# Sparse attention into a Swish feed-forward: batch 0 in two halves of queries, tiled scores and AV in every batch, block-mean rows copied by VectorE

## The chip, the cores and the metric

The program runs on one core of one Trainium2 chip. The metric is device time in microseconds (us) of one execution. Five instruction streams run side by side and meet through semaphores: TensorE (PE; its weight loads are shown apart as PEld), VectorE (DVE), ScalarE (ACT), GpSimd (POOL) and SyncE (SP). In this kernel POOL issues the loads from HBM, SP issues the copies inside SBUF, the transposes by DMA and the stores of the output; all of them share 16 DMA engines.

## The reference

Four batches, 8 heads, 768 positions, head dimension 64. Each query sees the keys nearer than 16 positions to it and, besides, 24 summary keys (the maximum over each block of 32 keys) whose values are the means over the blocks. The result goes through a feed-forward layer of 512 -> 2048 -> 512 with `h * sigmoid(beta * h)` between.

```
k_sum = k.reshape(B, H, nb, block, D).max(axis=3)        # block 32, nb 24
v_sum = v.reshape(B, H, nb, block, D).mean(axis=3)
scores_l = scale * q @ k.T                               # kept where |i - j| < 16
scores_s = scale * q @ k_sum.T + log(block)
a = softmax(concat([where(mask_l, scores_l, -1e9), scores_s]))
x = a @ concat([v, v_sum])                               # heads side by side: (3072, 512)
h = x @ w_in                                             # (3072, 2048)
out = (h / (1 + exp(-beta * h))) @ w_out                 # (3072, 512)
```

## The kernel before

**Tiling.** Two heads make a pair `g` (four pairs a batch). 64 queries and the 96 keys around them are one piece; a piece has 128 rows: 96 keys and, in 32 rows that the band leaves free, the 24 summary keys. Even and odd pieces (`par` 0 and 1) have their own images of K (`kw[:, 0]` and `kw[:, 1]`) and of V (`ve` and `vo`), shifted by 64 rows against each other. `vo` is a copy of `ve`, made by two DMAs of the SP queue (`copy_v`). The block means come from seven matmuls on `ve` (`prep_v`), are rounded into `vm`, and four DMAs a pair spread them into the free rows of `vo` and `ve` (L326). The two into `ve` have to wait until `copy_v` has read `ve`.

**Batch 0** runs before the feed-forward: for each pair its K and Q are transposed on TensorE (`prep_k`, `prep_q`), the block maxima are taken on VectorE (`rows_k`), then come the scores (L341 puts -30000 outside the band by a matmul with the identity, L345 adds q.k, two heads in the two 64-row halves of the array), the exponential on ScalarE, one pair later AV (L375, the odd pieces in the upper 64 columns of the array) and its normalisation (`norm0`), and two pairs later the transposition into `xT`. **Batches 1 to 3** do the same as side work of the batch before. There the two heads of a piece are kept apart by zeros in `q2`, so that a score piece is one matmul of 128x128 (L353), and AV is one of 128x130 (L380), half of whose output is not used; VectorE multiplies by the band (`mask`) and picks the valid halves in two instructions (L396). Batch 1 comes through TensorE transposes, batches 2 and 3 through DMA transposes (`cross`, and `rows_q` which spreads them into `q2`).

**Feed-forward.** Of each batch, 16 row tiles of the up projection (`h_tile`, eight matmuls of 384 columns each and one Silu), then six output tiles of the down projection in four parts of four matmuls (`o_part`). The weights are loaded once by POOL after the inputs of batch 0; `w_out` is scaled by 1/beta in 16 VectorE instructions (L225).

**What sets the order.** The program is written out by hand. Each engine executes in the order in which the instructions are emitted. The loop at the end keeps a list `main` (the feed-forward of batch b) and a list `side` of (position, function) with the attention of batch b+1; the side work is emitted before the entry of `main` whose number its position has reached. An engine whose next instruction waits lets nothing pass.

Of the kernel before, what the change touches and what calls it, by code (L numbers as in the profile page):

```python
# [12 lines left out]
def kernel(  # L13
# [10 lines left out]
    nc = tc.nc  # L24
# [54 lines left out]
    q2_bufs = [const.tile([P, nch, 2, 2, QT], bf16, name=f"q2{i}") for i in range(NKW)]  # L79
    qt_bufs = [const.tile([P, S], bf16, name=f"qt{i}") for i in range(2)]  # L80
# [39 lines left out]
    for g in range(2):  # L120
        load_hold("k", g, nc.sync)
        load_hold("q", g, nc.scalar)
# [6 lines left out]
    near = const.tile([P, 3, QT], bf16, name="near")  # L129
    nneg = const.tile([P, 3, QT], bf16, name="nneg")  # L130
    summ = const.tile([P, 1], f32, name="summ")
    band = const.tile([P, 2, nch, 2, QT], bf16, name="band")
    negband = const.tile([P, 2, nch, QT], bf16, name="negband")
# [18 lines left out]
    def clear_q(i):  # L152
        zero(q2_bufs[i][0:D, :, :, 1, :])
        zero(q2_bufs[i][D:P, :, :, 0, :])

# [6 lines left out]
    nc.vector.memset(A_col, 1.0 / block)  # L162
    make_identity(nc, identity)
    zero(A_avg)
    clear_v(0)
    select(A_col, -W, [[P, NC], [-block, nb]], 1)
    select(A_col, block - 1 + W, [[-P, NC], [block, nb]], -1)
    select(near, -1, [[0, 3], [-1, QT]], 1)
    select(near, 2 * W - 1, [[0, 3], [1, QT]], -1)
    select(near[:, 1], -W, [[0, QT]], 1)  # L170
    select(near[:, 2], D + W - 1, [[0, QT]], -1)
# [3 lines left out]
    load_v(0, 0)  # L175
    load_run("k", 0, 2)
    load_v(0, 1)
    load_run("q", 0, 2)
    load_v(0, 2)
    load_run("k", 0, 3)  # L180
    load_v(0, 3)
    load_run("q", 0, 3)

    nc.vector.tensor_copy(out=identity32[:], in_=identity[:])
    for t in vm_bufs:
        nc.vector.memset(t[:, :, D:VW], 1.0)
    clear_k(0)
    cast_hold("k", 0, nc.vector.tensor_copy)
    cast_hold("q", 0, nc.scalar.copy)
    clear_k(1)  # L190
    for s in SUM:
        nc.vector.tensor_copy(out=A_avg[:, :, s:s + nb], in_=A_col[:])
    nc.vector.tensor_scalar(out=near[:], in0=near[:], scalar1=summ[:, 0:1], scalar2=None, op0=ALU.max)
    nc.vector.tensor_scalar(out=bias[:, 0:1], in0=summ[:], scalar1=log_block, scalar2=None, op0=ALU.mult)
    nc.vector.tensor_scalar(out=nneg, in0=near, scalar1=1.0, scalar2=-NEG, op0=ALU.subtract, op1=ALU.mult)
    for lo, hi in ((0, D), (D, 0)):
        nc.vector.tensor_copy(out=bias[lo:lo + D, 1:2], in_=bias[hi:hi + D, 0:1])

    def spread(dst, src, bc):


        nc.vector.tensor_copy(out=dst[:, 0, 1:nch], in_=bc(src[:, 0], nch - 1))
        nc.vector.tensor_copy(out=dst[:, 0, 0:1], in_=bc(src[:, 1], 1))
        for lo, hi in ((0, D), (D, 0)):
            nc.vector.tensor_copy(out=dst[lo:lo + D, 1, 0:nch - 1], in_=bc(src[hi:hi + D, 0], nch - 1))
            nc.vector.tensor_copy(out=dst[lo:lo + D, 1, nch - 1:nch], in_=bc(src[hi:hi + D, 2], 1))

    spread(negband, nneg, lambda a, n: a[:, None, :].to_broadcast([a.shape[0], n, QT]))
# [12 lines left out]
    def make_band():  # L221
        spread(band, near, lambda a, n: a[:, None, None, :].to_broadcast([a.shape[0], n, 2, QT]))
# [46 lines left out]
    def prep_q(b, g, tag="t"):  # L269
        p = turn("q", b, g, tag)  # L270
        if b == 0:
            t = qt_bufs[g % 2]
            qt[(b, g)] = t
            nc.scalar.copy(out=t.rearrange("p (t j) -> p t j", j=J), in_=p.rearrange("p j t -> p t j"))
            return
        pv = p.rearrange("p j (m t) -> p m t j", t=QT // J)
        q2 = q2_bufs[(b * npair + g) % NKW].rearrange("p m r h (t j) -> p (m r) h t j", j=J)
        for h, copy in ((0, nc.scalar.copy), (1, nc.vector.tensor_copy)):
            copy(out=q2[h * D:(h + 1) * D, :, h], in_=pv[h * D:(h + 1) * D])  # L279

    def cross(b, g):
# [4 lines left out]
        qt[(b, g)] = qk_pool.tile([P, nch, P], bf16, name="q_tr", tag="q_tr")  # L286
        nc.sync.dma_start_transpose(out=qt[(b, g)][:], in_=qn.rearrange("p c h d -> p (c h d)"))

    def rows_k(b, g):
        kw = kw_of(b, g)  # L290
        cv = nc.vector.tensor_copy
        cv(out=kw[:, 1, 0:nch, 64:P], in_=kw[:, 0, 0:nch, 64:P])  # L292
        cv(out=kw[:, 1, 0:nch, 0:32], in_=kw[:, 0, 1:NC, 0:32])
        flat = kw[:, 0].rearrange("p c f -> p (c f)")[:, W:W + S].rearrange("p (n f) -> p n f", f=block)
        half = at_pool.tile([P, nb, block // 2], bf16, name="half", tag="half", bufs=2)
        nc.vector.tensor_max(out=half[:], in0=flat[:, :, 0:block // 2], in1=flat[:, :, block // 2:block])
        km = at_pool.tile([P, nb], bf16, name="km", tag="km")
# [160 lines left out]
    for i in range(2, NKW):  # L458
        clear_k(i)
# [122 lines left out]
```

## Time and profile before

| | us |
|---|---|
| median of 3 runs (lowest to highest) | 261.42 (260.54 to 261.93) |
| the profiled execution, its own time | 259.94 |
| its span in the trace | 258.1 |
| PE busy | 222.5 (86%) |
| ACT busy | 120.1 (47%) |
| DVE busy | 114.6 (44%) |
| POOL busy | 64.2 (25%) |

The span is the time from the first to the last instruction of the trace; the execution's own time has 1.84 us more around it. Busy time is the union of an engine's instructions. The page cuts the span into 40 slices of 6.45 us and gives a digit for each. The chain of waits follows the work that ended last backwards from instruction to releaser. It gives 68% to PE, 16% to DMA and 10% to DVE. By line it names the two projections (L427 30%, L442 27%), the spreading of the block means into `ve` (8%), AV of batches 1 to 3 (3%) and the copies of `ve` into `vo` (3%).

### The profile page before, as it was taken

How to read it: one execution, taken by the hardware profiler on the slowest of the kernel's cores; microseconds unless marked ns; L12 is line 12 of the kernel's file. 1: busy time of each engine (PE TensorE's matmuls, PEld its weight loads, DVE VectorE, ACT ScalarE, POOL GpSimd, SP SyncE). 2: the span in 40 equal slices, each digit the busy share in tenths (PEclk: the TensorE clock that was granted, in tenths of full speed). 3: DMA queues.
4: the chain of work that ended last, by engine and by line, in shares of the span. 5: the costliest groups of instructions: out<-in, count | busy, mean ns of one | idle time of the engine just before them, and what ended most of it. 6: DMA issues, size and time to landing. Idle time of an engine off the chain costs nothing.

```text
span 258.1 us, 4624 instructions
## 1 busy us (share of the span) xinstructions
PE 222.5 (86%) x1809; PEld 131.9 (51%) x1809; DVE 114.6 (44%) x324; ACT 120.1 (47%) x140; POOL 64.2 (25%) x90
## 2 busy tenths in 40 slices
PE   0495764289999889899996999999999999999994
PEld 0353543256566545456662665566655545664441
DVE  3932532068174887704335876062378720001221
ACT  2554404036788424146666433566675418662000
POOL 8962121740198620006638000000000000000000
PEclk9999955589999999999999999999999999999999
DMA  6999999999099957139999942565434441000122
GB/s 190 185 181 200 192 204 196 177 178 50 0 105 143 179 65 112 55 95 147 151 157 166 151 122 74 142 138 97 83 52 118 96 118 43 0 0 10 74 81 81
DMA packets 95669, 29.73 MB, mean 115 GB/s; under 512 B 83856, under 2 KB 91808, under 8 KB 95648
## 3 DMA queue, kind: packets, MB, share of 16 engines
q0 software_dynamic: 56768, 12.85, 59.9%
q1 hardware_dynamic: 38464, 15.81, 29.6%
q10 hardware_dynamic: 416, 0.79, 1.1%
q8 instruction: 14, 0.23, 0.4%
q14 instruction: 7, 0.06, 0.1%
HBM read 27.27 MB, written 6.29 MB: 130 GB/s over the span
## 4 chain that ended last, share of the span: by engine, by line
PE 68%; DMA 16%; DVE 10%; ACT 2%; issue 1%; SPq 1%; DVEq 0%; ACTq 0%
PE h_ps L427 30%; PE o_ps L442 27%; DMA ve<-vm 8%; PE av_ps L380 3%; DMA vo<-ve 3%; PE s_ps L353 2%; DMA kw<-k_nat 2%; DMA hold_k<-in_k_dram 2%; DVE x_nat L396 2%; DMA vo<-vm 2%; PE vm_ps L319 2%; PE av_ps L375 1%; DVE q L279 1%; DVE km L298 1%; PE px L411 1%
## 5 line engine op out<-in xcount | busy, mean ns | idle before, releaser
L442 PE MATMUL o_ps<-w_out_sb,h_sb 128*128 128x512 bf16 x384 | 89.3, 379 | 0.1
L427 PE MATMUL h_ps<-xT,w_in_sb 128*128 128x384 bf16 x512 | 86.8, 328 | 0.6 <-DVE xT L412 0.6
L431 ACT ACTIVATE h_sb<-h_ps,beta_sb 128x768 bf16<-128x768 f32 x64 | 57.1, 900 | 38.6 <-PE h_ps L427 38.5
L427 PEld LDWEIGHTS <-w_in_sb 128*128 128x128 bf16 x512 | 49.6, 98 | 33.3 <-issue 1.6
L442 PEld LDWEIGHTS <-h_sb 128*128 128x128 bf16 x384 | 35.9, 98 | 36.8 <-issue 0.3
L354 ACT ACTIVATE attn<-s_ps,bias 128x768 bf16<-128x768 f32 x24 | 21.4, 900 | 19.2 <-PE s_ps L353 16.2
L396 DVE TENSOR_TENSOR x_nat<-av_ps,r 64x384 bf16<-64x384 f32 x48 | 26.6, 555 | 1.2
L446 ACT COPY o_sb<-o_ps 128x512 f32<-128x512 f32 x18 | 10.5, 585 | 30.6 <-PE o_ps L442 25.6
L98 POOL DMA_DIRECT2D k_nat<-in_k_dram x16 | 13.4, 844 | 42.0 <-DMA kw<-k_nat 27.1
L446 DVE COPY o_sb<-o_ps 128x512 f32<-128x512 f32 x6 | 4.2, 692 | 41.8 <-issue 28.1
L292 DVE COPY kw<-kw 128x384 bf16<-128x384 bf16 x16 | 5.0, 313 | 36.3 <-DMA kw<-k_nat 33.4
L105 POOL DMA_DIRECT2D ve<-in_v_dram x16 | 17.0, 1060 | 5.8 <-DVE x_nat L387 2.7
L375 PE MATMUL av_ps<-ve,attn 128*64 128x65 bf16 x48 | 4.0, 240 | 12.4 <-DMA ve<-vm 12.4
L359 DVE TENSOR_TENSOR attn<-attn,band 128x768 bf16<-128x768 bf16 x24 | 13.3, 556 | 1.8 <-ACT attn L354 1.2
L380 PEld LDWEIGHTS <-attn 128*128 128x128 bf16 x144 | 10.1, 97 | 7.6 <-DVE attn L359 2.8
L98 POOL DMA_DIRECT2D q_nat<-in_q_dram x16 | 13.2, 837 | 2.9 <-DMA q_tr<-q_nat 2.6
L353 PE MATMUL s_ps<-q,kw 128*128 128x128 bf16 x144 | 11.9, 219 | 1.2 <-DVE x_nat L396 1.2
L261 PE MATMUL pk<-identity,k_run 96*64 96x96 bf16 x128 | 5.5, 244 | 8.4 <-DVE k_run L116 6.7
L375 PEld LDWEIGHTS <-attn 128*64 128x64 bf16 x96 | 5.3, 154 | 13.3 <-issue 12.3
L319 PE MATMUL vm_ps<-ve,A_avg 128*128 128x128 bf16 x112 | 10.4, 241 | 1.7 <-DMA ve<-in_v_dram 1.7
L267 ACT COPY kw<-pk 128x768 bf16<-128x768 bf16 x8 | 6.4, 796 | 11.0 <-PE pk L261 9.7
L347 ACT ACTIVATE attn<-s_ps,bias 128x768 bf16<-128x768 f32 x8 | 7.1, 899 | 8.9 <-PE s_ps L345 8.9
(76 smaller groups left out, 180.8 us busy)
## 6 DMA issues: line engine op xcount, KB each, us to landing
out_dram<-o_sb SPq DMA_DIRECT2D x24, 256.0 KB, 2.3
ve<-in_v_dram POOLq DMA_DIRECT2D x12, 192.0 KB, 7.0
w_in_sb<-in_moe_w_in_dram POOLq DMA_DIRECT2D x4, 512.0 KB, 14.8
w_out_sb<-in_moe_w_out_dram POOLq DMA_DIRECT2D x4, 512.0 KB, 22.3
vo<-ve SPq DMA_DIRECT2D x16, 97.5 KB, 5.4
k_nat<-in_k_dram POOLq DMA_DIRECT2D x16, 96.0 KB, 5.6
q_nat<-in_q_dram POOLq DMA_DIRECT2D x16, 96.0 KB, 5.6
k_run<-in_k_dram POOLq DMA_DIRECT2D x6, 192.0 KB, 8.5
```

The source lines that it names most:

```text
L98: nc.gpsimd.dma_start(out=t[:, :, h], in_=(k_row if nm == "k" else q_row)[b, g, :, h])
L105: nc.gpsimd.dma_start(out=ve_bufs[b % 2][:, lo:hi, 0:D], in_=src)
L319: nc.tensor.matmul(vm_ps[:], A_avg[:, c, :], ve[:, lo:lo + nch + 1:nch, 0:D], start=(c == 0), stop=(c == NC - 1))
L353: nc.tensor.matmul(sv[:, m // HM, m % HM], kw[:, m, :], q2[:, m, par], start=True, stop=True)
L354: nc.scalar.activation(out=a.rearrange("p (k j) h f -> p k (j h f)", k=2), in_=big[:, :, 0:w], func=ACTF.Exp, bias=bias[:, par:par + 1], s ...
L359: nc.vector.tensor_mul(out=a, in0=a, in1=band[:, par])
L380: nc.tensor.matmul(ov[:, m // HM, m % HM], a[:, m], vt[:, m:m + nch + 1:nch], start=True, stop=True)
L396: nc.vector.tensor_mul(out=x[par * QT:(par + 1) * QT, :, hh, :].rearrange("p (k j) d -> p k j d", k=2), in0=ov[lo:lo + D, :, :, hh, 0:D], ...
L427: nc.tensor.matmul(big[:, kk, 0:MG], w_in_sb[:, ki, ni * P:(ni + 1) * P], xT[b][:, ki, kk * MG:(kk + 1) * MG], start=(ki == 0), stop=(ki = ...
L431: nc.scalar.activation(out=h_bufs[(b, ni // 8)][:, ni % 8, :].rearrange("p (k m) -> p k m", k=2), in_=big[:, :, 0:MG], func=ACTF.Silu, sca ...
L442: nc.tensor.matmul(o_ps[:], h_bufs[(b, ni // 8)][:, ni % 8, ms * P:(ms + 1) * P], w_out_sb[:, ni, :], start=(ni == 0), stop=(ni == k2 - 1))
L446: (nc.scalar.copy if b + 1 < B else nc.vector.tensor_copy)(out=o_sb[:], in_=o_ps[:])
```

## The change

Four things are done together.

1. The feed-forward's loop runs over five units instead of four batches: the first half of the queries of batch 0, its second half, and batches 1 to 3. Before unit 0 only the first half of batch 0's queries goes through scores, AV and `xT` (`scores_half(g, 0)`: three even and three odd pieces of both heads in one PSUM tile). The second half's rows of K and V are made at the start of unit 0, and its scores, AV and transposes stand in unit 0's down projection. A unit of half a batch takes two row tiles of the up projection at once (`h_group`) and has three output tiles. The side list is ordered by planned time (`GT`, `OT`) instead of by the number of an entry.
2. Scores and AV are tiled in all batches: twelve score matmuls with 64 rows of the array each instead of six of 128x128, and 24 AV matmuls of 128x65 that use 64 columns of the array instead of twelve of 128x130. `q2`, its zeros and `rows_q` are gone; Q goes into `qt_bufs`. One `norm` serves both `par`.
3. The block-mean rows of batches 0 and 1 are written by VectorE (`rows_v`, four copies a pair); batches 2 and 3 keep the four DMAs.
4. Smaller moves: K and Q of the first two pairs are loaded in halves on two queues, the band comes from one 64-wide pattern (`negedge` for the two ends), constants are prepared in another order, and the batch 2 loads follow unit 0.

```diff
+    def rows_v(b, g, m0=0, m1=nch, dma=False):
+        for par, t in ((0, ve_bufs[b % 2]), (1, vo_bufs[b % 2])):
             lo = SUM[par]
+            vm = vm_bufs[g][lo:lo + 32]
+            dst = t[lo:lo + 32, PC * g:PC * (g + 1)].rearrange("p (h c) e -> p h c e", h=2)
             for h in range(2):
-                c = PC * g + nch * h
-                nc.sync.dma_start(out=t[lo:lo + 32, c:c + nch], in_=vm[lo:lo + 32, h, None].to_broadcast([32, nch, VW]))
+                if dma:
+                    nc.sync.dma_start(out=dst[:, h], in_=vm[:, h, None].to_broadcast([32, nch, VW]))
+                else:
+                    nc.vector.tensor_copy(out=dst[:, h, m0:m1], in_=vm[:, h, None].to_broadcast([32, m1 - m0, VW]))
...
+    def scores_half(g, hf):
+        kw, q = kw_of(0, g), qt_bufs[g]
...
+        for h in range(2):
+            nc.tensor.matmul(sv[:, h], identity, negband[:, :, None, :].to_broadcast([P, 2, HM, QT]), start=True, stop=False)
+            nc.tensor.matmul(sv[:, h, hf, hf * (HM - 1)], identity, negedge[:, hf], start=False, stop=False)
+        for par in range(2):
+            for m in range(HM):
+                for h in range(2):
+                    lo = h * D
+                    nc.tensor.matmul(sv[:, h, par, m], kw[lo:lo + D, par, hf * HM + m, :], q[lo:lo + D, hf * HM + m, par],
+                                     start=False, stop=(par == 1 and m == HM - 1))
...
     def scores(b, g, par):
...
-            for m in range(nch):
-                nc.tensor.matmul(sv[:, m // HM, m % HM], kw[:, m, :], q2[:, m, par], start=True, stop=True)
+        for m in range(nch):
+            for h in range(2):
+                lo = h * D
+                nc.tensor.matmul(sv[:, h, m], kw[lo:lo + D, par, m, :], q[lo:lo + D, m, par], start=True, stop=True)
...
+    def av(key, m0, n):
...
+        for par, t in ((0, ve_bufs[b % 2]), (1, vo_bufs[b % 2])):
+            for m in range(n):
                 for h in range(2):
-                    nc.tensor.matmul(ov[par * QT:(par + 1) * QT, h, m], a[:, m, h], vt[:, h * nch + m], start=True, stop=True)
-            return
-        o = ps.tile([P, 2, 512], f32, name="av_ps", tag="big", bufs=3)
-        ov = o[:, :, 0:HM * 2 * VW].rearrange("p k (j h e) -> p k j h e", h=2, e=VW)
-        for m in range(nch):
-            nc.tensor.matmul(ov[:, m // HM, m % HM], a[:, m], vt[:, m:m + nch + 1:nch], start=True, stop=True)
+                    nc.tensor.matmul(ov[par * QT:(par + 1) * QT, h, m], a[:, par, m, h], t[:, PC * g + nch * h + m0 + m],
+                                     start=True, stop=True)
...
+    units = [(0, 0, 1), (0, MG, 1)] + [(b, 0, 2) for b in range(1, B)]
+    NG = [k2 // (2 // w) for _, _, w in units]
...
+        if u == 0:
+            at_time(0.5, make_band)
             for g in range(npair):
+                at_time(1.0 + 0.3 * g, rows_k, 0, g, HM, nch)
+                at_time(1.1 + 0.3 * g, rows_v, 0, g, HM, nch)
+                t = up + 1.7 * g
+                at_time(t, scores_half, g, 1)
+                at_time(t + 2.6, av, (0, g, 1), HM, HM)
+                at_time(t + 2.7, norm, (0, g, 1), HM)
...
+            for n in range(k2):
+                at_time(3.0 + 0.3 * n, scale_w_out, n)
```

Three places show what moves. SP's queue in batch 0, before, from the spreading of the first pair's means (`vm_115`; `ve_81` and `vo_83` are batch 0's images of V) to that of the second:

```order
L326 DMA vo_83<-vm_115 32x6x65 x2
L326 DMA ve_81<-vm_115 32x6x65 x2
L311 DMA vo_83<-ve_81 64x780
L312 DMA vo_83<-ve_81 32x780
L326 DMA vo_83<-vm_116 32x6x65 x2
L326 DMA ve_81<-vm_116 32x6x65 x2
```

and now, at the fourth and last pair of copies of batch 0 (the three before it stand right in front of it); `vo_84` and `ve_82` are batch 1's:

```order
L294 DMA vo_83<-ve_81 64x780
L295 DMA vo_83<-ve_81 32x780
L434 DMA out_dram<-o_sb 128x512 x3
L294 DMA vo_84<-ve_82 64x780
L295 DMA vo_84<-ve_82 32x780
```

The eight DMAs of block means between the copies of two pairs are gone from the queue, and batch 1's copies now stand behind unit 0's three output stores.

VectorE in batch 0, before, around the third pair's K rows (`kw_87`):

```order
L321 CAST vm_116<-vm_ps 128x2x64
L292 COPY kw_87<-kw_87 128x6x64
L293 COPY kw_87<-kw_87 128x6x32
L296 TENSOR_TENSOR half<-kw_87 128x384
L298 TENSOR_REDUCE km<-half 128x24
L300 COPY kw_87<-km 128x6x24 x2
L386 RECIPROCAL r<-av_ps 128x12
L387 TENSOR_TENSOR x_nat<-av_ps,r 128x2x6x64
```

and now:

```order
L314 COPY ve_81<-vm_117 32x195 x2
L314 COPY vo_83<-vm_117 32x195 x2
L279 TENSOR_TENSOR half<-kw_87 128x384
L281 TENSOR_REDUCE km<-half 128x24
L286 COPY kw_87<-kw_87 128x3x64
L287 COPY kw_87<-kw_87 128x3x32
L289 COPY kw_87<-km 128x3x24 x2
L374 RECIPROCAL r_410<-av_ps 128x6
L375 TENSOR_TENSOR x_nat_409<-av_ps,r_410 128x2x3x64
L303 CAST vm_118<-vm_ps 128x2x64
```

The row copies of the first pair (`vm_117` now) stand in VectorE's stream ahead of the third pair's K rows, and the row copies and normalisation cover three pieces instead of six.

VectorE at the end of its preparations for the first down projection, before:

```order
L138 MEMSET q_92 64x12x32 x2
L225 TENSOR_SCALAR w_out_sb<-w_out_sb,inv_beta 128x512 x15
L279 COPY q_89<-pq 64x12x64
L225 TENSOR_SCALAR w_out_sb<-w_out_sb,inv_beta 128x512
L292 COPY kw_85<-kw_85 128x6x64
```

and now:

```order
L286 COPY kw_88<-kw_88 128x3x64
L287 COPY kw_88<-kw_88 128x3x32
L289 COPY kw_88<-km 128x3x24 x2
L314 COPY ve_81<-vm_120 32x195 x2
L314 COPY vo_83<-vm_120 32x195 x2
L217 TENSOR_SCALAR w_out_sb<-w_out_sb,inv_beta 128x512 x16
L374 RECIPROCAL r_854<-av_ps 128x6
L375 TENSOR_TENSOR x_nat_853<-av_ps,r_854 128x2x3x64
```

In front of the scaling of `w_out` now stand the second half's K and V rows of all four pairs (the fourth is shown) instead of the zeros of `q2`, and the second half's first normalisation follows it.

## Rows read from the trace of the kernel before

**Rows 1.** The page's part 2: 40 slices, tenths of full clock, of DMA time.

```profile
PEclk9999955589999999999999999999999999999999
DMA  6999999999099957139999942565434441000122
```

**Rows 2.** The chain of waits, 0 to 55 us: start, length, what.

```profile
27.14 7.38 DMA vo<-ve
...
50.05 1.24 PE av_ps L375 x23
51.29 2.88 PE h_ps L427 x12
```

**Rows 3.** Waits over the whole span: us in total, times, longest.

```profile
PE av_ps L375 <- DMA ve<-vm: 12.4, 8, 4.0
...
PE av_ps L380 <- DVE attn L359: 2.2, 1, 2.2
```

**Rows 4.** The timeline of SP: first and last copy pair of batch 0.

```profile
11.10 0.56 SPq L311 DMA_DIRECT2D vo<-ve  x1
...
35.93 0.56 SPq L311 DMA_DIRECT2D vo<-ve  x1
```

**Rows 5.** The timeline of POOL: start, length, [idle before <-releaser].

```profile
18.82 1.50 POOL L235 DMA_DIRECT2D w_out_sb<-in_moe_w_out_dram  x2 [1.10 <-DMA ve<-in_v_dram]
```

**Rows 6.** The instructions on `w_out_sb`, 0 to 80 us: durations, first and last start.

```profile
L235 POOL DMA_DIRECT2D w_out_sb<-in_moe_w_out_dram x4: 740/740/742, 15.8 to 19.6; - x4
...
DMA to landing us min/median/max: 20.1/22.3/25.6
```

**Rows 7.** The chain of waits, whole span, at the borders of stages.

```profile
55.16 13.81 PE h_ps L427 x84
68.97 0.46 PE pk L261 x16
...
112.88 5.20 PE h_ps L427 x32
118.08 0.40 PE vm_ps L319 x7
...
144.47 0.35 PE av_ps L380 x6
144.81 0.34 PE s_ps L353 x6
...
164.12 5.20 PE h_ps L427 x32
...
212.71 20.80 PE h_ps L427 x128
233.51 20.73 PE o_ps L442 x96
```

**Rows 8.** The timeline of PE: a pair's scores in batch 0, around 29 us.

```profile
29.20 0.35 PE L345 MATMUL s_ps<-qt,kw 64*128 64x64 bf16 x12
29.48 0.50 PE L341 MATMUL s_ps<-negband,identity 128*128 128x384 bf16 x2
29.91 0.35 PE L345 MATMUL s_ps<-qt,kw 64*128 64x64 bf16 x12
```

**Rows 9.** Groups by form: busy us, mean ns of one, idle before.

```profile
L396 DVE TENSOR_TENSOR x_nat<-av_ps,r 64x384 bf16<-64x384 f32 x48 | 26.6, 555 | 1.2
...
L300 DVE COPY kw<-km 128x144 bf16<-128x144 bf16 x32 | 5.3, 227 | 0.6
...
L387 DVE TENSOR_TENSOR x_nat<-av_ps,r 128x768 bf16<-128x768 f32 x4 | 3.8, 958 | 0.1
```

**Rows 10.** The timeline of DVE: one pair's K rows; the scaling of `w_out`.

```profile
29.24 0.25 DVE L292 COPY kw<-kw 128x384 bf16<-128x384 bf16 x1
...
30.50 0.30 DVE L300 COPY kw<-km 128x144 bf16<-128x144 bf16 x2
...
61.16 4.03 DVE L225 TENSOR_SCALAR w_out_sb<-w_out_sb,inv_beta 128x512 bf16<-128x512 bf16 x15
```

More of the change, by code (lines that the diff above doesn't have):

```diff
@@ L162 @@
     nc.vector.memset(A_col, 1.0 / block)
-    make_identity(nc, identity)
[L164 to L171, printed above, removed]
+    clear_k(0)
+    clear_v(0)
+    zero(negedge)
+    nc.vector.memset(negedge[0:W, 0], NEG)
+    nc.vector.memset(negedge[0:32, 1], NEG)
+    zero(negedge[0:W, 1])
+    zero(A_avg)
+    make_identity(nc, identity)
+    select(near, -1, [[-1, QT]], 1)
+    select(near, 2 * W - 1, [[1, QT]], -1)
     select(summ, -SUM[0], [[0, 1]], 1)
@@ L175 @@
     load_v(0, 0)
+    select(A_col, -W, [[P, NC], [-block, nb]], 1)
+    select(A_col, block - 1 + W, [[-P, NC], [block, nb]], -1)
     load_run("k", 0, 2)
@@ L221, in make_band @@
     def make_band():
-        spread(band, near, lambda a, n: a[:, None, None, :].to_broadcast([a.shape[0], n, 2, QT]))
+        for par in range(2):
+            for lo, hi in ((0, D), (D, 0)):
+                src = near[hi:hi + D] if par else near[lo:lo + D]
+                nc.vector.tensor_copy(out=band[lo:lo + D, par], in_=src[:, None, None, :].to_broadcast([D, nch, 2, QT]))
+        zero(band[0:W, 0, 0])
+        zero(band[0:32, 1, nch - 1])
+        nc.vector.tensor_copy(out=band[0:W, 1, nch - 1], in_=near[D:D + W, None, :].to_broadcast([W, 2, QT]))
     def scale_w_out(n):
@@ L270, in prep_q @@
         p = turn("q", b, g, tag)
[L271 to L274, printed above, removed]
-            return
[L276 to L279, printed above, removed]
+        flat = qt_bufs[g].rearrange("p m r f -> p (m r f)")
+        nc.scalar.copy(out=flat.rearrange("p (t j) -> p t j", j=J), in_=p.rearrange("p j t -> p t j"))
     def cross(b, g):
@@ L318, in prep_v @@
             lo = PC * g + c
-            nc.tensor.matmul(vm_ps[:], A_avg[:, c, :], ve[:, lo:lo + nch + 1:nch, 0:D], start=(c == 0), stop=(c == NC - 1))
-        vm = vm_bufs[g]
-        nc.vector.tensor_copy(out=vm[:, :, 0:D], in_=vm_ps[:])
-        for par, t in ((1, vo), (0, ve)):
+            nc.tensor.matmul(vm_ps[:], A_avg[:, c, :], ve_bufs[b % 2][:, lo:lo + nch + 1:nch, 0:D],
+                             start=(c == 0), stop=(c == NC - 1))
+        nc.vector.tensor_copy(out=vm_bufs[g][:, :, 0:D], in_=vm_ps[:])
@@ L330, in scores @@
     def scores(b, g, par):
-        kw = kw_of(b, g)[:, par]
+        kw, q = kw_of(b, g), qt_bufs[g]
         if par == 0:
@@ L408, in x_transpose @@
             return
-        px = psum([P, S], bf16, "px", tag)
-        for c in range(nch):
+        px = psum([P, n * P], bf16, "px", tag)
+        for c in range(n):
             nc.tensor.transpose(px[:, c * P:(c + 1) * P], x[:, c].rearrange("p h d -> p (h d)"), identity)
-        nc.vector.tensor_copy(out=xT[b][:, g, :], in_=px[:])
+        copy(out=xT[b][:, g, m0 * P:(m0 + n) * P], in_=px[:])
     MG = 384
@@ L488 @@
         load_v(1, g)
[L489 to L497 removed]
+    rows_v(0, npair - 1, 0, HM)
+    x_transpose((0, npair - 2, 0), 0, HM, "t", act)
+    av((0, npair - 1, 0), 0, HM)
+    norm((0, npair - 1, 0), HM)
+    h_group(0, 0, range(k1 - 1))
+    h_group(0, 1, range(k1 - 1))
+    x_transpose((0, npair - 1, 0), 0, HM, "t", dve)
```

323 lines of the change are left out of this document (149 added, 174 removed).

## The prediction

> **What bounds the kernel now.** I read the page's slices first, then the chain of waits, then the queues behind the waits it names. TensorE is the bound from 55 us to the end: from there the chain is one matmul after another, and the last two batches' projections run without a gap [rows 7]. Before 55 us it is not. The granted clock shows five tenths, the 1.2 GHz level, in the sixth to eighth slice, while the DMA engines are nine tenths busy [rows 1]. The chain there alternates between two DMAs, `vo<-ve` and `ve<-vm`, and AV waited 12.4 us for the second kind alone [rows 2, 3]. The reason is SP's order. The spreading of a pair's block means into `ve` waits until `copy_v` has read `ve`, 7.4 us after its issue [rows 2], and behind the waiting DMA stands the next pair's copy. So the first and last of four copies lie at 11.1 and 35.9 us, 8.3 us a pair [rows 4], although V had landed long before: POOL's wait on its last piece ended at 18.8 us [rows 5]. The first projection streams from 55.2 us [rows 7]. Call that point F.
>
> **Before unit 0.** The new queue holds only the four copies, so each starts when its V lands. The first still starts near 11.1; two issues (0.6 each, [rows 4]) and 6 to 7.4 us later its data lies there, at about 18.3. Then VectorE makes four row copies of 195 elements. The trace has no such copy, so I bound it: a 768-element operation that reads PSUM takes 958 ns, 1.25 ns an element, which gives 0.24; a broadcast copy of 144 elements takes 227 ns [rows 9], which gives 0.31 at the same rate; twice as fast an access would give 0.16. I take 0.27, four are 1.1. First AV: 19.4 us.
>
> After that VectorE's own stream sets the pace, because TensorE and ScalarE wait for it in turn. A pair costs the row copies 1.1, the K rows 1.6 (from 29.24 to 30.80, [rows 10]), half a normalisation 0.7 (half of 958 ns and a reciprocal, an estimate) and a cast of 0.3 (as a reciprocal, likewise): 3.7 us. What waits in VectorE for a copy now holds up the next pair's K rows, which was SP's part before. The last copy lands at 18.8 + 1.2 + 7.4 = 27.4, its rows are ready at 28.5; the pairs themselves need 19.4 + 3 x 3.7 = 30.5, so that copy is hidden. From the last AV to F the trace has 5.1 us (50.05 to 55.16); with half an AV, half a transpose and half a copy I take 4.0. F = 34.5, a gain of 20.7.
>
> **Unit 0.** Half the attention that was in front now stands inside the feed-forward. From F: 52 up-projection matmuls at 0.164 (13.81 / 84) 8.5; 48 down-projection matmuls at 0.216 (20.73 / 96) 10.4 [rows 7]; four half scores, each 0.43 for the two masking matmuls, 0.28 for the twelve tiled ones [rows 8] and 0.07 for the edges (128 more columns at the same rate), 3.1; four half AVs 1.5 (below); three transposes 0.5. That is 24.0. Then `w_out` must be scaled. In front of the scaling VectorE now has the band (about 2.4: four copies at half of 958 ns and small ones) and the second half's rows, 4 x (0.5 + 1.1), so it starts at F + 9.1; 16 instructions at 0.27 (4.03 / 15, [rows 10]) end at F + 13.4. TensorE is ready for the first part at F + 9.3, and gets it at F + 10.5. I charge 1.2. `w_out` itself landed no later than 19.6 + 25.6 = 45.2 us [rows 6], before the last scaling at 47.5, so this transfer stays hidden; if F came 3 us earlier, it would not, and half of that would be lost again. Unit 0 ends at E = 34.5 + 25.2 = 59.7.
>
> **Unit 1** carries batch 1's attention. 64 up-projection matmuls 10.5, 48 down 10.4, K, Q and mean matmuls 4 x (0.46 + 0.46 + 0.40) 5.3 [rows 7], eight tiled scores at 0.28 instead of 0.34 [rows 7, 8] 2.2, four AVs 3.0, transposes 1.3: 32.7. Here a new wait comes in. Batch 1's copies stand on SP behind unit 0's last output, so the first lands at about E + 8.5 (1 us for the result, 1.2 for two issues, 6 to 7 for landing). Only then VectorE makes batch 1's first rows (four of 390 elements, 0.47 each, 1.9), the next pair's K rows 1.6 and its mean cast 0.3: E + 12.3. TensorE comes to the Q transposes that need this cast's PSUM at about E + 9.9 by its own sum. I charge 2.4. Unit 1 ends at 59.7 + 35.1 = 94.8. The same point before, the end of batch 0's down projection, is 112.9 [rows 7]. So 18.1 of the 20.7 are left.
>
> **AV.** 24 tiled matmuls instead of twelve. Full, at 2.4 GHz, a pair's two calls take 2 x 0.35 [rows 7]. Tiled rows exist only in batch 0 at 1.2 GHz: 1.24 [rows 2]. Half of that, 0.62, is the lower end, 1.24 the upper. I take 0.75, the ratio by which the tiled scores fell being nearer to half than to one; half a call is 0.38. Over twelve pairs that is +0.6; the ends are -1.0 and +6.5, with half AVs +7.5.
>
> The page "TensorEngine Tiling (Array Packing)" of the Trainium skill, section Restrictions and Gotchas, speaks against this part: column tiling cannot be combined with Fast Weight Load. The page "TensorE: Matmul & The Clock Gate", section LDWEIGHTS, gives a load by its columns, 64 / 1.2 = 53 ns here whatever the array's clock. By that rule 24 loads in turn take an estimated 1.28 us a pair also at 2.4 GHz, and the whole comes out near 247; no row before shows it at that level. It is the first rival below, whose own price is the trace's 1.24.
>
> **Units 2 to 4.** Batch 1's feed-forward took 51.2 us, 2.2 of it AV waiting for the masks, behind the K rows of the last DMA transpose [rows 3, 7]. `rows_q` (which also waited for a DMA) is gone from VectorE's stream, and AV comes later: I leave 0.5 of the wait. Matmuls: 20.8 + 20.7 + 4 x 0.40 + 8 x 0.28 + 4 x 0.75 + 0.3 = 48.7. So 49.2, a gain of 2.0. Batch 2's took 48.6, new 48.4, a gain of 0.2. The last is unchanged. VectorE saves much here, with one normalisation of 958 ns for four of 555 [rows 9], but its time lies beside matmuls and is worth nothing more.
>
> **Sum:** -18.1 - 2.0 - 0.2 = -20.3. From 259.9 (span 258.1 and 1.84 around it) that is 239.6; the median of the runs shown is 1.5 above that execution. I say 240.
>
> **Rivals.**
> - *The tiled AV keeps its cold price* of 1.24 a pair. +0.5 x 14 over my value: 247. For it: no row shows the opposite, and batch 0's 24 matmuls follow each other within one column tile. Against it: the K transposes, which use 64 columns too, take 0.46 for 16 at the high clock [rows 7], 29 ns each.
> - *The copies at the start stretch.* The DMA engines are full until 50 us [rows 1], and four copies now run beside the weights. If each takes twice 7.4 us, F moves by some 7 us: 247. Against it: block-mean DMAs, sixteen in batch 0, leave the same engines.
> - *More than that:* rows copied at the fast rate, TensorE at the high clock already in batch 0, unit 1 without its wait: up to -7, 233.
> - *The clock falls.* Short tiled pieces and waits fill the first two units. If TensorE drops to 1.2 GHz there, as it did in the slices after 32 us [rows 1], each us of matmuls costs another; 20 us of the 57 in units 0 and 1 eat up the gain, and if all of unit 0's 24 run so, the time is 264, slower. Against it: from 55 us on all slices are at the full level, those with waits too [rows 1].
> - *The change doesn't reach its end:* a wait that replaces SP's, VectorE standing at a copy with the K rows behind it, at the old pace of 8.3 a pair. Then F is 48 and the time 253. The copies no longer wait for each other, so I see little for it.
>
> **Chances.** Forecast, 234 to 243: 0.60. Cold AV 0.13, stretched copies 0.10, better than forecast 0.08, old pace 0.05, clock 0.04. The first three and the fourth lie within 232 to 249, which is the range; a part of the forecast's own tail and the last two lie outside. Half a per cent, 1.3 us, is about what a measurement of this kernel can tell from no change. Faster by more: 0.94; within: 0.02; slower: 0.04.
>
> **What the profile will show.** Right: four copy pairs on SP between 11 and 21 us, the stream of up-projection matmuls from 33 to 36 us, VectorE's row copies near 0.27, a short gap in front of the first down projection, VectorE waiting for `vo<-ve` near 66 us and TensorE about 2 us behind it, AV of a pair near 0.75, unit 2 from 95 us on. Wrong: copies of 10 us or more, AV above 1.0, clock digits under nine after 40 us, a last stage of another length than 45 us, or a wait in batches 2 and 3 that wasn't there.

## The result, and the profile after

The changed kernel takes 243.6 us (median of four, 243.0 to 245.3) against 261.7 for the kernel before: ratio 0.932, 95% interval 0.926 to 0.939. The forecast was 240, range 232 to 249. Ratios and intervals, here and below, are taken over the executions within 1.5% of a kernel's fastest one. The execution that was profiled took 245.33 us (span 243.6); the forecast's own sum for one execution was 239.6.

The page's part 2, answering to [rows 1], shows one slice of 6.1 us under the full clock. The three slices at half clock before 55 us are gone, and a new low one stands at 122 to 128 us.

```profile
PEclk9999999999999999999979999999999999999999
DMA  6999999999999563999999244845542230001212
```

The timeline of SP (start, length) has only the four copy pairs in batch 0, 2 to 4 us apart, where [rows 4] had 8.3; the sixteen row transfers, four a pair, are gone:

```profile
12.28 0.57 SPq L294 DMA_DIRECT2D vo<-ve  x1
...
15.26 0.50 SPq L294 DMA_DIRECT2D vo<-ve  x1
...
19.60 0.49 SPq L294 DMA_DIRECT2D vo<-ve  x1
...
21.84 0.48 SPq L294 DMA_DIRECT2D vo<-ve  x1
```

The chain of waits at the borders of the stages, answering to [rows 2, 7]. TensorE streams from 34.22 (before 55.16); unit 2 reaches from 93.46 to 148.03, with the last pair's K transpose on the chain in its middle.

```profile
34.22 8.61 PE h_ps L410 x52
...
58.80 0.97 PE h_ps L410 x6
...
80.67 0.78 PE av_ps L365 x24
...
93.46 2.06 PE h_ps L410 x12
...
114.34 6.88 DMA kw<-k_nat
...
148.03 5.20 PE h_ps L410 x32
...
198.02 20.80 PE h_ps L410 x128
218.82 20.73 PE o_ps L429 x96
```

| us | forecast | measured | best version below |
|---|---|---|---|
| F, first up projection streams | 34.5 | 34.2 | 33.2 |
| unit 0 | 25.2 | 24.6 | 24.9 |
| unit 1 | 35.1 | 34.7 | 33.6 |
| unit 2 | 49.2 | 54.6 | 48.7 |
| unit 3 | 48.4 | 50.0 | 47.5 |
| unit 4 to the span's end | 45.4 | 45.6 | 45.6 |

So the miss of 5.7 in this execution lies in units 2 (5.4) and 3 (1.6); the start and units 0 and 1 were 1.3 shorter than forecast. In the groups by form (busy us, mean ns, idle before) the row copies cost about what was estimated: 0.24 to 0.25 us (0.27) and 0.39 to 0.47 (0.47):

```profile
L314 DVE COPY vo<-vm 32x390 bf16<-32x390 bf16 x8 | 3.4, 465 | 0.1
L314 DVE COPY ve<-vm 32x195 bf16<-32x195 bf16 x16 | 3.4, 250 | 4.3 <-DMA q_run<-in_q_dram 4.2
```

Unit 2 on VectorE (timeline, idle and its releaser in brackets). It stands 5.47 us at the last pair's K transpose. The mean cast of that pair and the masks come behind it in the stream:

```profile
121.24 0.36 DVE L279 TENSOR_TENSOR half<-kw 128x384 bf16<-128x384 bf16 x1 [5.47 <-DMA kw<-k_nat]
...
122.90 0.29 DVE L303 CAST vm<-vm_ps 128x128 bf16<-128x128 f32 x1
123.10 1.02 DVE L355 TENSOR_TENSOR attn<-attn,band 128x768 bf16<-128x768 bf16 x2
```

TensorE's waits (total, times, longest), answering to [rows 3]. The 12.4 us of AV for `ve<-vm` are gone. The first down projection of unit 2 now waits for that cast, since in the kernel both take the same PSUM buffers (tag `t`) and the means still occupy one:

```profile
PE o_ps L429 <- DVE vm L303: 1.9, 1, 1.9
```

Behind that wait the granted clock fell to its 1.2 GHz level. In the windows (stretch, length, PE, PEld, DVE, ACT and POOL busy, clock, DMA share) TensorE is idle for most of 121 to 123, then at 0.88, 0.50 and 0.77 of full clock. By these three rows 2 x (0.12 + 0.50 + 0.23) = 1.7 us are lost.

```profile
121.00:123.00 2.00, 0.33 (x2) 0.05 (x1) 1.73 (x7) 0.89 (x2) 1.25 (x2) 1.00 2.04 175
123.00:125.00 2.00, 1.76 (x18) 0.77 (x18) 1.12 (x3) 0.41 (x1) 0.66 (x2) 0.88 2.20 121
125.00:127.00 2.00, 2.00 (x20) 0.89 (x19) 0.00 (x0) 0.49 (x1) 1.38 (x2) 0.50 2.71 129
127.00:129.00 2.00, 2.00 (x32) 1.08 (x28) 1.30 (x3) 0.00 (x0) 0.00 (x0) 0.77 1.72 149
```

### The profile page after: what moved, and what is told of

Same layout as the page of the kernel before. It is cut to its first block, busy times and chain, and to the rows that moved or that the text cites. A ratio compares the mean times of both kernels' runs of the same rounds, so it can differ in the third digit from the quotient of the medians.

```text
span 243.6 us, 5218 instructions
## 1 busy us (share of the span) xinstructions
PE 222.9 (91%) x2113; PEld 126.9 (52%) x2113; DVE 96.0 (39%) x322; ACT 126.8 (52%) x169; POOL 66.4 (27%) x88
## 4 chain that ended last, share of the span: by engine, by line
PE 71%; DMA 11%; SPq 7%; POOL 4%; DVE 4%; issue 2%; ACT 1%; DVEq 0%; POOLq 0%
PE o_ps L429 33%; PE h_ps L410 23%; DMA kw<-k_nat 7%; PE av_ps L365 5%; DMA q_run<-in_q_dram 4%; SPq L312 4%; PE s_ps L349 2%; PE vm_ps L301 2%; POOL ve L105 1%; PE px L389 1%; PE s_ps L327 1%; SPq L295 1%; SPq L294 1%; PE pk L253 1%; PE pq L253 1%
## 5 line engine op out<-in xcount | busy, mean ns | idle before, releaser
L417 ACT ACTIVATE h_sb<-h_ps,beta_sb 128x768 bf16<-128x768 f32 (+1 forms) x80 | 59.3, 773 | 27.0 <-PE h_ps L410 26.9
L350 ACT ACTIVATE attn<-s_ps,bias 128x768 bf16<-128x768 f32 x24 | 21.5, 901 | 22.4 <-PE s_ps L349 22.1
L279 DVE TENSOR_TENSOR half<-kw 128x384 bf16<-128x384 bf16 x16 | 5.7, 358 | 47.4 <-DMA kw<-k_nat 42.4
L433 ACT COPY o_sb<-o_ps 128x512 f32<-128x512 f32 x18 | 10.5, 585 | 23.7 <-PE o_ps L429 22.9
L365 PEld LDWEIGHTS <-attn 128*64 128x64 bf16 x384 | 13.4, 117 | 8.9 <-issue 7.9
L375 DVE TENSOR_TENSOR x_nat<-av_ps,r 128x768 bf16<-128x768 f32 (+1 forms) x20 | 15.9, 797 | 0.7
L374 DVE RECIPROCAL r<-av_ps 128x12 f32<-128x12 f32 (+1 forms) x20 | 4.3, 216 | 24.6 <-PE av_ps L365 24.6
L365 PE MATMUL av_ps<-ve,attn 128*64 128x65 bf16 x192 | 10.6, 204 | 2.2 <-DVE ve L314 2.2
L336 ACT ACTIVATE attn<-s_ps,bias 128x384 bf16<-128x384 f32 x16 | 8.3, 577 | 4.9 <-PE s_ps L333 4.9
L365 PE MATMUL av_ps<-vo,attn 128*64 128x65 bf16 x192 | 10.7, 203 | 0.0
L349 PEld LDWEIGHTS <-kw 64*128 64x128 bf16 x288 | 5.5, 95 | 9.3 <-issue 9.1
## 6 DMA issues: line engine op xcount, KB each, us to landing
w_in_sb<-in_moe_w_in_dram POOLq DMA_DIRECT2D x4, 512.0 KB, 14.6
```

The costliest lines, as they stand in the source:

```text
L350: nc.scalar.activation(out=a.rearrange("p m h f -> p h m f"), in_=sv, func=ACTF.Exp, bias=bias[:, par:par + 1], scale=scale)
L365: nc.tensor.matmul(ov[par * QT:(par + 1) * QT, h, m], a[:, par, m, h], t[:, PC * g + nch * h + m0 + m], start=True, stop=True)
L375: nc.vector.tensor_mul(out=x.rearrange("p m h d -> p h m d"), in0=ov[:, :, :, 0:D], in1=r[:, :, :, None].to_broadcast([P, 2, n, D]))
L417: nc.scalar.activation(out=hb.rearrange("p (k m) -> p k m", m=MG), in_=big[:, j:j + w, 0:MG], func=ACTF.Silu, scale=beta_sb[:, ni:ni + 1])
L433: (nc.scalar.copy if u + 1 < len(units) else nc.vector.tensor_copy)(out=o_sb[:], in_=o_ps[:])
```

## The experiments

Theories: SP's alternation set the start, and rows written by VectorE end it; unit 2 lost to VectorE's order and the clock behind it; and tiles cost something at each change to and from the whole array. Rivals are named with each run. The kernel before was run beside every group of runs (medians 261.7 to 264.0), and the changed kernel itself, run again, came to 0.913 after 0.932. Versions that lie closer than that are compared by the lengths of their units.

**Row copies alone, in the kernel before.**

```diff
-                nc.sync.dma_start(out=t[lo:lo + 32, c:c + nch], ...)
+                eng = nc.vector.tensor_copy if b < 2 else nc.sync.dma_start
+                eng(out=t[lo:lo + 32, c:c + nch], ...)
```

> The kernel before with one part of the change alone: the block-mean rows of batches 0 and 1 are written by VectorE instead of the sixteen SP transfers a batch; batch 0 stays whole, AV and scores stay as they were. Theory (SP's alternation of copies and row transfers set the start): the four copies follow each other as V lands, VectorE's work of a pair (four row copies of 390 elements 1.9, K rows 1.6, a whole normalisation 1.3, a cast 0.3 = 5.1 us) becomes the pace, so the first projection streams at 19.4 + 3 x 5.1 + 5.1 = 40 us instead of 55.2, and the time is 261.5 - 15 = 246 to 249. Rival (the halving of batch 0 gave most of the gain, the row copies little): the stream begins at 48 us or later and the time is 254 or more.

Measured 251.0, ratio 0.952 (0.946 to 0.957). The chain has the stream at 40.59, as forecast:

```profile
40.59 13.81 PE h_ps L428 x84
```

14.6 us are won there, but batch 0's feed-forward ends only 12.4 us earlier (100.49 for 112.88): VectorE, with rows, the spreading of Q and four-part normalisations in one place, keeps TensorE waiting (5.0 us for normalisations in this stretch, for 3.6 before, and 1.1 for a mean cast). Batch 1's feed-forward has a wait of 3.5 for a mask, for 2.2 before, and is 3.8 longer (100.49 to 155.56). The row copies alone carry 11 of the 18 us; the rest needs the other parts.

**The change without the row copies.**

```diff
-                if dma:
+                if True:
```

> The changed kernel with only that part undone: the block-mean rows of batches 0 and 1 go by SP transfers again, batch 0 stays in two halves, AV and scores stay tiled. Theory: the alternation of about 8 us a pair is back on SP, last copy near 37 us, first projection at 48 to 52 us instead of 34.2, and unit 1 (33 us for batch 1's four pairs on the same queue) gets up to 5 us longer: 256 to 264. Rival (the halving gave the gain): the stream begins before 40 us and the time stays under 250.

Measured 272.0, slower than before: 1.036 (1.032 to 1.041). The stream begins at 63.07. The waits say why, and the chain shows the cycle of one pair: rows land, AV runs, and only behind it the next pair's means, from which the next rows are made (they land at 35.6).

```profile
PE av_ps L365 <- DMA ve<-vm: 23.9, 8, 7.8
PE av_ps L365 <- DMA vo<-vm: 5.6, 8, 1.4
```

```profile
20.86 5.60 DMA vo<-vm
26.50 0.43 PE av_ps L365 x5
26.94 0.88 PE vm_ps L301 x7
```

So this run doesn't measure the halving: the new order was made for rows of half a microsecond, and with transfers it pays a latency per pair. The last run of all mends that.

```diff
         scores_half(g, 0)
-        if g >= 1:
-            rows_v(0, g - 1, 0, HM)
+        prep_v(0, g)
+        rows_v(0, g, 0, HM)
```

> The changed kernel with the block-mean rows of all batches by SP transfers, as in the run that took 272, but with each pair's mean matmuls and its rows one pair earlier in batch 0's order (in front of the AV of the pair before, not behind it). In the run that took 272 TensorE waited 29.5 us at AV for these rows, because the means of pair g stood behind the AV of pair g-1, so that each pair paid a transfer's latency in full. Theory 1 (that order, made for rows written by VectorE, is why halving without them is slower than the kernel before): the waits fall to about 20, SP's alternation of 8 us a pair remains, the first projection streams at 48 to 52 us instead of 63.1, time 257 to 262. Theory 2 (the halves lose by SP transfers in any order, because the second half's eight pairs of row transfers stand in front of unit 0's output and batch 1's copies): the stream begins at 48 to 55 but units 0 and 1 lengthen, time 265 or more.

Measured 257.3, 0.975 (0.970 to 0.980); the stream begins at 44.74 and AV's waits are 15.7.

```profile
PE av_ps L365 <- DMA ve<-vm: 11.0, 4, 7.8
...
PE av_ps L365 <- DMA vo<-vm: 4.7, 7, 2.2
```

Theory 1 holds, with an earlier stream than its 48 to 52: in an order of its own the halving, with the rest of the change, gains without row copies too (6.8 us). These take 10.5 us more off the start (44.74 to 34.22), and 2.4 off unit 1, which takes 37.1 here. The two parts alone, 11.4 and 6.8 us, add up to the 18.1 of the whole change within 0.1.

**AV in turn between the two column tiles.**

```diff
-        for par, t in ((0, ve_bufs[b % 2]), (1, vo_bufs[b % 2])):
-            for m in range(n):
-                for h in range(2):
+        for m in range(n):
+            for h in range(2):
+                for par, t in ((0, ve_bufs[b % 2]), (1, vo_bufs[b % 2])):
```

> The changed kernel with the 24 AV matmuls of a pair in another order: even and odd pieces in turn, so that neighbours in the queue use the lower and the upper 64 columns of the array, instead of twelve in one column tile and then twelve in the other. Theory 1 (the 0.78 us a pair are two column tiles run one after the other; where neighbours lie in different tiles they start 14 ns apart instead of 30): 0.40 us a pair, 0.2 a half, so 12 x 0.38 + 4 x 0.2 = 5.4 less, 238. Theory 2 (the price is the loading of 24 sets of weights in turn or the output's bank, whatever their order): AV stays at 0.75 to 0.8 and the time at 243.6 within 0.5.

Measured 239.6, 0.909 (0.903 to 0.915); AV is 0.50 a pair in the chain. TensorE's timeline shows neighbours starting together, a couple every 30 ns; in one tile after the other, one starts every 30 ns.

```profile
87.17 0.19 PE L365 MATMUL av_ps<-ve,attn 128*64 128x65 bf16 x1
87.17 0.19 PE L365 MATMUL av_ps<-vo,attn 128*64 128x65 bf16 x1
87.20 0.20 PE L365 MATMUL av_ps<-ve,attn 128*64 128x65 bf16 x1
87.20 0.20 PE L365 MATMUL av_ps<-vo,attn 128*64 128x65 bf16 x1
```

Theory 1 holds, at 0.28 instead of 0.38 a pair. Units 1 and 3 are 1.1 and 0.9 shorter. Unit 2 gained nothing (91.19 to 145.64, 54.5): TensorE only reaches the same wait earlier (3.0 us). In this execution the start also came 1.2 earlier, as it can without any edit (below).

**Batch 3's loads later in the order.**

```diff
-                    at_time(1.0 + 4.5 * g, load_next, nxt + 1, g)
+                    at_time((up if u > 1 else 0.0) + 1.0 + 4.5 * g, load_next, nxt + 1, g)
```

> The changed kernel with one thing moved: batch 3's loads go out during unit 2's down projection, as in the kernel before, instead of during its up projection. Theory 1 (the transposes by DMA of batch 2's K and Q, the last of which took 6.9 us, share the DMA engines with these loads): the last one lands within 3 us, VectorE's wait of 5.5 us before the last pair's K rows and the 1.9 us of TensorE behind it are gone, the clock doesn't fall at 121 to 130 us, unit 2 falls from 54.6 to about 50 and the time to 239. Theory 2 (the transposes are late because of what stands before them on SP): the last K transpose lands 27 to 28 us after the unit's start as now, time 243 to 244.5.

Measured 242.6, 0.924 (0.918 to 0.929), and inconclusive: POOL waits for free buffers alone, so the loads went out where they had before (the third pair's K at 114.56 us, for 114.34). The last K transpose took 6.6 us. TensorE's wait for the cast was 1.4 us here instead of 1.9, the clock did not fall, and unit 2 took 52.6; since nothing was moved, this is how much executions differ by themselves. The edit that really moves the loads gives them buffers:

```diff
-    qk_pool = ctx.enter_context(tc.tile_pool(name="qk", bufs=4))
+    qk_pool = ctx.enter_context(tc.tile_pool(name="qk", bufs=7))
```

> The changed kernel with seven instead of four buffers for each of the loaded K and Q, so that three of batch 3's four pairs are loaded as soon as V's buffer is free, around 81 to 98 us, and not while batch 2's K and Q are transposed by DMA. (In the run with the later place in the order these loads went out at the same times as before, since POOL waits only for free buffers.) Theory 1 (contention): the last K transpose, 6.9 us from issue to landing, lands in about 3; it lies there 23 to 25 us after the unit's start instead of 27.8, TensorE's wait of 1.9 us and the fall of the clock go, 239 to 240. Theory 2 (the transposes are slow behind the transfers of their own queue, copies and block-mean rows): landing stays above 6 us and the time at 243 to 244.

Measured 243.2, 0.922 (0.915 to 0.930). Neither theory as stated: the last transpose did land in 2.79 us (chain), but the earlier ones got slower (a median of 7.1 for the four K transposes, for 6.0), and the last lies there 28.2 us after the unit's start. The unit took 53.2. Contention seems to move with the loads; the landing stays where it was.

```profile
118.47 2.79 DMA kw<-k_nat
```

**VectorE's order in units 2 and 3.**

```diff
-                    at_time(t, max_k, nxt, g)
-                    at_time(t, rows_k, nxt, g)
+                    tk = t if g + 1 < npair else up + 3.0
+                    at_time(tk, max_k, nxt, g)
+                    at_time(tk, rows_k, nxt, g)
```

> The changed kernel, where in units 2 and 3 the last pair's block maxima and K rows stand in VectorE's stream behind the mean cast of that pair and the first pair's two band multiplications, instead of ahead of them; nothing else moves. Theory 1 (the loss in unit 2 is VectorE's order: it stands at the last K transpose, 5.5 us, and the mean cast and masks that TensorE needs for its first down projection and first AV stand behind it): TensorE's wait of 1.9 us on the cast goes, the clock stays up at 121 to 130 us, unit 2 falls from 54.6 to about 50.5, the time to 239 to 240. Theory 2 (the transposes by DMA set the end of the unit's attention, wherever VectorE waits): the wait moves to the last pair's scores, unit 2 stays above 53 and the time at 243 to 244.

Measured 240.5, 0.914 (0.908 to 0.919). Unit 2 is 51.0 (91.23 to 142.22 in the chain), TensorE's wait for the cast is gone from it and the clock is whole. VectorE's timeline has the masks ahead of the K rows, and the transpose has landed when it comes to them:

```profile
91.23 2.06 PE h_ps L410 x12
...
142.22 5.20 PE h_ps L410 x32
```

```profile
119.10 0.56 DVE L355 TENSOR_TENSOR attn<-attn,band 128x768 bf16<-128x768 bf16 x1 [0.49 <-ACT attn L350]
119.57 0.35 DVE L279 TENSOR_TENSOR half<-kw 128x384 bf16<-128x384 bf16 x1
```

Theory 1 holds for the unit. The time by itself would not show it, since all but one of the changed kernel's own executions spread over 239.6 to 246.0.

**Full AV in batches 1 to 3.**

```diff
+        if b > 0:
+                    nc.tensor.matmul(ov[:, m // HM, m % HM], a[:, par, m], t[:, lo:lo + nch + 1:nch], start=True, stop=True)
```

> The changed kernel with the old AV for batches 1 to 3: twelve matmuls of 128x130 on the whole array and the normalisation in four 64-row instructions a pair; scores stay tiled, batch 0 stays as it is. Theory 1 (tiled AV costs 0.78 a pair and about 0.1 more at the next full matmul, the full one 2 x 0.35 and no switch): 12 x 0.18 = 2.2 less, 241 to 242. Theory 2 (VectorE's longer normalisation, 2.2 + 0.6 us a pair for 1.3, delays masks and transposes more than that): 244 to 247. If tiled and full are worth the same: 243 to 244.

Measured 243.4, 0.926 (0.919 to 0.932): the same. TensorE has 0.70 a pair and no change of form at AV, but VectorE's four-part normalisations get onto the chain at the end of unit 1:

```profile
95.32 0.56 DVE x_nat L389
```

The sameness is a sum of unlike parts: unit 1 is 1.4 longer (36.1), units 2 (51.8, with a wait of only 0.6 for the cast and a whole clock) and 3 (49.0) are shorter than in the profiled execution of the changed kernel.

**The price of a change of form, by itself.**

```diff
+            for ms, (kind, n) in enumerate((("full", 0), ("full", 2), ("col", 2), ("row", 2), ("col", 6), ("full", 6))):
+                for p in range(4):
+                    at_time(up + (4 * ms + p) * OT - 0.01, probe, kind, n)
```

> A price by itself: in the last unit's down projection, where TensorE runs without a gap, small matmuls whose result nobody reads stand in front of each of the four parts of an output tile: none for tile 0, two on the whole array (128x64) for tile 1, two that use 64 columns each for tile 2, two that use 64 rows each for tile 3, six of 64 columns for tile 4, six whole ones for tile 5. Theory 1 (every change between the whole array and a tile costs about 0.1 us once, however many matmuls follow): tile 1 costs 4 x 0.06 us over tile 0's 3.46, tiles 2 and 3 0.4 us more than tile 1, tile 4 as much more than tile 5. Theory 2 (the 0.10 to 0.11 us seen behind tiled pieces are only how the end of the last matmul is modelled): tiles 1, 2 and 3 last equally long within 0.1 us, tiles 4 and 5 too.

The timeline of TensorE, two neighbouring places each for two whole matmuls (`128*128`), two of 64 columns (`128*64`) and two of 64 rows (`64*128`):

```profile
222.18 0.22 PE L566 MATMUL sw_ps<-identity 128*128 128x64 bf16 x2
...
223.11 0.22 PE L566 MATMUL sw_ps<-identity 128*128 128x64 bf16 x2
...
226.16 0.22 PE L568 MATMUL sw_ps<-identity 128*64 128x64 bf16 x2
...
227.28 0.22 PE L568 MATMUL sw_ps<-identity 128*64 128x64 bf16 x2
...
230.63 0.20 PE L570 MATMUL sw_ps<-identity 64*128 64x64 bf16 x2
...
231.73 0.20 PE L570 MATMUL sw_ps<-identity 64*128 64x64 bf16 x2
```

The pitch is 0.93, 1.12 and 1.10; without small matmuls it is 0.864 (4 x 20.73 / 96). So two whole ones cost 0.06, two tiled ones 0.17 to 0.19 more for going in and out again. Over the four places of a tile that is 0.7 to 0.8 us, where theory 1 had 0.4: the price is paid in both directions. With six, columns take 0.14 more than whole ones (pitches 1.18 and 1.04), but being two tiles in turn they need only half the 0.18 themselves. It is a cost per change, not per matmul, and theory 2 is out. This agrees with the Trainium skill, page "TensorEngine Tiling (Array Packing)", section Tiling Modes, by which changing the mode drains the engine; it gives no price. Below, a run of tiled matmuls between two whole ones is called a burst.

**Together**, beside the changed kernel once more.

> The changed kernel once more, unaltered, beside the two runs that follow, so that they are compared on one chip: 243 to 246.

Median 243.9; one execution of 756.8 us stands outside, the others lie between 239.6 and 246.0. The ratio is 0.913 (0.907 to 0.919), from the two shortest, 239.6 and 241.3. Unit 2 took 55.4 in the trace.

> The changed kernel with both edits that helped alone: AV matmuls in turn between the two column tiles, and the last pair's K rows behind the first masks on VectorE in units 2 and 3. If the two gains lie in different places (AV 0.78 to 0.50 a pair, twelve pairs and four halves, 3.9 us; unit 2's wait and clock, 3 to 3.5 us) they add up: 7 less than the changed kernel, 237. If the shorter AV only makes TensorE reach the same waits earlier, as in unit 2 of the run with the first edit alone, the gain is 4 to 5.

Measured 237.3, 0.900 (0.896 to 0.904). By the ratios this is only 3.6 us less than the changed kernel, by the medians 6.6, so the time doesn't decide. In the units the two gains add up: unit 2 is 49.9, unit 3 48.6, each 1.1 below the run with the order alone.

```diff
+                if nxt > 1:
+                    t = up + 3.6 * g
+                    for par in range(2):
+                        at_time(t, scores, nxt, g, par)
+                        at_time(t + 1.0, mask, nxt, g, par)
+                    t += 3.6 - lag - 0.05
```

> The run before it, with one thing more: in units 2 and 3 a pair's two score calls follow each other and the AV of the pair before stands right in front of them, so that between two full matmuls of the down projection there is one burst of tiled matmuls a pair instead of three. Theory 1 (a change between the whole array and a tile costs 0.1 us each way, 0.19 for both in the probe of the last unit): two bursts fewer for each of eight pairs, 8 x 0.4 = 3.0 less than the run before at most, 2 to 3 if the change from row tiles to column tiles costs as much. Theory 2 (the 0.1 is gone only where other work covers it, or VectorE's masks become late with two scores at once): no gain, within 0.7 us.

Measured 233.5, 0.888 (0.883 to 0.892), the best of all and clear of both kernels. In the chain a pair's 24 score matmuls stand directly behind the AV of the pair before, one burst instead of three:

```profile
120.13 0.50 PE av_ps L365 x24
120.63 0.46 PE s_ps L349 x24
121.24 3.40 PE o_ps L429 x15
```

Units 2 and 3 shrink by 1.15 each, 2.3 in sum (theory 1's 2 to 3). The medians differ by 3.7, more than that; the start, which varies by some 3 us from run to run, lies in both. The lengths in the chains of the profiled executions:

| us | changed, twice | AV in turn | order | both | joined |
|---|---|---|---|---|---|
| F | 34.2, 31.5 | 33.1 | 32.0 | 31.0 | 33.2 |
| unit 1 | 34.7, 34.7 | 33.6 | 34.7 | 33.6 | 33.6 |
| unit 2 | 54.6, 55.4 | 54.5 | 51.0 | 49.9 | 48.7 |
| unit 3 | 50.0, 49.8 | 49.1 | 49.8 | 48.6 | 47.5 |

## Why the prediction came out as it did

**The start: right in its cause, met in its number by luck.** SP's alternation was the cause; the runs with and without row copies show the step by itself. But the sum behind F, a first AV at 19.4 us and then 3 x 3.7 us at VectorE's pace, is not what the trace has. The first AV came at 20.07, the others at 25.74, 28.70 and 30.74 (timeline). By the chain VectorE's first row copies waited here for a load of Q, in seven of the ten executions named below for the first `vo<-ve`; and from 23 to 30 us the chain runs through TensorE:

```profile
10.43 9.29 DMA q_run<-in_q_dram
...
23.01 0.85 PE pk L253 x16
...
69.04 0.46 PE pk L253 x16
```

Sixteen transposes take 0.85 us there and 0.46 at 69.04, although the clock column reads 1.00 in both places; so that column does not show every stretch in which TensorE is slow. F within 0.3 also belongs to this execution alone. In the ten profiled executions whose start is written the same F lies between 31.0 and 34.2, always earlier than forecast. The difference lies in the first landing: VectorE's first row copy starts at 16.2 to 19.8 us, and F comes 13.9 to 15.3 us behind it.

**Unit 0: right in length, not in content.** The charged wait of 1.2 us did not come. VectorE's scaling began at 42.31 (timeline), the first part at 43.49 (chain), 1.2 us behind, and no part had to wait:

```profile
42.31 4.29 DVE L217 TENSOR_SCALAR w_out_sb<-w_out_sb,inv_beta 128x512 bf16<-128x512 bf16 x16
```

```profile
43.49 1.83 PE o_ps L429 x8
```

The 1.83 for eight matmuls, 0.10 above 8 x 0.216, show what stands in its place: the change from the tiled scores in front of them, which I had not priced. In the whole unit the down projection takes 11.1 in the chain, for the 10.4 of the sum. The trace of before had shown this price, in the line behind the K transposes of [rows 7], which are tiled too; eight of these matmuls take 8 x 0.164 = 1.31 otherwise:

```profile
69.43 1.42 PE h_ps L427 x8
```

**Unit 1: the same.** I charged 2.4 us for `copy_v` behind unit 0's output, at landings of 6 to 7.4 us taken from the start. The copies were issued from 59.95 on, 1.15 behind the unit's start (forecast 1), but landed in 2.8 (median), and the rows followed the cast without a wait (VectorE's timeline):

```profile
64.82 0.51 DVE L303 CAST vm<-vm_ps 128x128 bf16<-128x128 f32 x1
65.39 1.02 DVE L314 COPY ve<-vm 32x390 bf16<-32x390 bf16 x2
```

In its place the chain has 0.8 more in the down projection (11.2 for 10.4) and 0.4 in the up projection behind K and Q transposes (1.41 for 1.31, four times), both the price of bursts, a wait of 0.6 for ScalarE's first copy of K, and 0.3 more in AV and means. That is 2.1 that I had not charged, about the size of the wait that I had. Two errors cancelled.

**Tiled AV and scores: right in price, incomplete.** 0.78 for 0.75, and 0.28. The trace at the high clock shows 0.78 a pair, and 0.50 in turn. The Trainium skill, page "TensorEngine Tiling (Array Packing)", section Restrictions and Gotchas, says that column tiling and Fast Weight Load exclude each other. That the 24 loads then run in turn, for an estimated 1.28, was my own step, and it is not borne out in that size. What the section Tiling Modes of the same page of the Trainium skill says, that tiles load and multiply independently, is what the run with alternating tiles shows. What the step left out is the price of getting into tiles and back, 0.19 a burst. About half of it stands in the measured pieces (two calls of scores take 0.28 each, joined 0.46); the 0.10 behind each burst stood in no term.

**Unit 2: the term that was mis-sized.** "I leave 0.5 of the wait." The step saw that `rows_q` left VectorE's stream, but not that the mean cast and masks still stood behind the last K rows, and that the last K transpose would land later: 6.88 us after its issue, for 5.67 in the chain of before, and 27.8 us after the unit's start, for 25.6. SP's queue has a part in this: it issues almost without a break from 93.88 to 114.34 (timeline), and eight row transfers stand in front of this transpose, as before; no run takes them away.

```profile
132.82 5.67 DMA kw<-k_nat
```

Mis-sized by 5.4: with VectorE's order mended the unit takes 51.0, so 3.6 are the wait (1.9) and the clock behind it (1.7). The execution with a wait of 1.4 and a whole clock, 52.6, fits this. Of the 1.8 left the chain of the mended run has 1.2 in the down projection (twelve bursts at 0.10), 0.9 at the unit's start, where the last transposition of batch 1 and the copy behind it were charged with only 0.3, and 0.1 in AV, less the 0.5 that I had charged for the wait. With AV at 0.50 and one burst a pair it is 48.7.

**Unit 3: 1.6 long**, 1.2 of it the twelve bursts again; mending the order leaves 49.8, one burst a pair with AV in turn gives 47.5.

**Rivals.** "The clock falls" was priced for units 0 and 1 and came, for some 5 us, in unit 2; a clock digit under nine after 40 us was one of the signs named for a wrong step. "The old pace" is what the row transfers in the new order gave, and worse. The stretched copies did not come: batch 0's copies landed in 5.1 to 7.4 us. The 243.6 lies in the range but 0.6 outside the 234 to 243 that had the 0.60, and no rival had named its cause.

What stays open is why most of the transposes by DMA take 6 to 8 us in unit 2 whichever way the loads lie, and what sets the time of the first landing, and with it the 3 us by which the start varies.

## What to carry to other kernels

Count the changes between whole-array and tiled matmuls, not only the matmuls: here each burst cost 0.19 us, and joining bursts (1.15 in each of two units) and taking the two column tiles in turn (1.1 in each of three) gave 5.6 us, where the choice between tiled and full AV gave nothing. When a wait is removed, read the stream of the engine that waited to its end: what stands behind the next late operand is late too. An order that suits a short operation can lose everything when that operation becomes a transfer again, so an undone part has to get its own order before it is compared.

## What the runs showed that I had not expected

Halving without row copies was slower than the kernel before (272.0), though each part gains by itself once it has its own order. A place 21 us later in the planned order did not move POOL's loads by a microsecond; only buffers did. And with the loads out of the way the last transpose took 2.8 us instead of 6.9, and yet the unit took 53.2, no less than the 52.6 of an execution whose loads had not moved.
